# Crossbar transposes in an attention layer, from batch 2 on instead of batch 3

## The chip, the cores and the metric

One core of one Trainium2 chip. The metric is the device time of one execution in microseconds (us). Before the change was tried, the kernel took 334.17 us (median of 3 runs, 334.12 to 334.18). Every run in this document is in the fast state, in which executions of one kernel usually lie within 0.3%. The changed kernel's lie a little wider than the kernel before's; the experiments come back to that.

The engines go by their names in the profile: TensorE is PE, its weight loads PEld, VectorE is DVE, ScalarE ACT, GpSimd POOL and SyncE SP. PSUM is the memory that TensorE writes its results to. A DMA "lands" when its data has arrived; its landing time is counted from its issue.

## The reference

Attention over 8 batches of 8 heads, 576 positions, 64 dimensions per head, then a two-layer network over its result.

```
scores = q @ k^T / 8                       per batch and head
heads 0-3: keep 0 <= i - j < 32            ("local")
heads 4-7: keep j <= i, j = i (mod 32)     ("strided")
x   = softmax(scores) @ v                  -> [4608 tokens, 512]
h   = x @ w_in                             512 -> 2048
out = (max(h,0) + alpha*min(h,0)) @ w_out  2048 -> 512, float32
```

## The kernel before

The 4608 tokens go through the two layers in nine chunks of 512, each with 16 pieces of the first layer (64 matmuls of 512 columns) and 16 of the second (64 more). The attention is cut into pieces and threaded between them. Each batch has four head pairs, two local and two strided, numbered `g = 4*batch + pair`. `DX` is the batch from which the crossbar (a transposing DMA) takes over transposes from TensorE:

```
DX = 3
...
P.dx = P.b >= DX and P.strided      # q and k through the crossbar
P.xd = P.b >= DX and P.hp < 3       # results of pairs 0, 1, 2 through the crossbar
```

On the TensorE path q and k are transposed in eight matmuls each, plus four for the tail of the sequence, into PSUM, and DVE or ACT copies them on (`transpose_piece`, `tails`). On the crossbar path POOL loads q and k (casting to 16 bits) and SP issues the transposes:

```
def load_d(b):                                   # POOL queue, software DMA
    for nm, src in (("q", q), ("k", k)):
        keep(nc.gpsimd.dma_start(qks[nm][0:72], src[b, 4:8]...))
def transpose_d():                               # SP queue, crossbar
    for nm, dst in (("q", qTs[1]), ("k", kTs[1])):
        ...
        keep(nc.sync.dma_start_transpose(o, qks[nm]...))
```

`qks` is one pair of buffers, so a batch's load must wait until the crossbar has read the batch before. Results: on TensorE, `x_piece` transposes the pair into PSUM and a copy puts it into `xT`, the input of the first layer. On the crossbar path:

```
def x_dma(P):
    if P.strided:                                # pair 2: a scratch tile, then ACT reorders
        P.xs = xpool.tile([128, 8, 80], F16, ...)
        keep(nc.sync.dma_start_transpose(P.xs, P.x16[0:80, :]))
    else:                                        # pairs 0, 1: straight into xT
        keep(nc.sync.dma_start_transpose(xT[:, P.hp, ...], P.x16[0:96, 0:768]))
def x_copy(P):
    keep(nc.scalar.copy(xT[:, P.hp, ...], P.xs[:, :, 0:72]...))
```

Pair 3 of each batch stays on TensorE in both kernels; its copy on ACT is the last thing before the next chunk. The steps for pair `g` of batch `c` are tied to the attention pieces:

```
if lastp:
    if 4 * DX <= g - 1 < npair and pairs[g - 1].xd:
        x_dma(pairs[g - 1])
    if g % 4 == 0 and DX <= c < B:
        transpose_d()
    if g % 4 == 2 and DX <= c and c + 1 < B:
        load_d(c + 1)
    if g % 4 == 2 and c + 2 < B:
        load_v(c + 2, False)
if copyp and 4 * DX <= g - 2 < npair and pairs[g - 2].xd and pairs[g - 2].strided:
    x_copy(pairs[g - 2])
```

ACT's instructions stand in program order in the traces below: a wait of `x_copy` for the crossbar holds up whatever ACT has behind it. In the changed kernel an exponential whose scores were there at about 100.3 us ran at 102.86, behind such a wait.

The softmax here doesn't subtract the row's maximum and nothing guards it: scores larger than these inputs give would overflow.

Of the kernel before, what the change touches and what calls it, by code (L numbers as in the profile page):

```python
# [31 lines left out]
def kernel(  # L32
# [51 lines left out]

    NE = 6

    DX = 3
    qTs = [cpool.tile([128, 2, 672], F16, name=f"qT{i}") for i in range(2)]
    kTs = [cpool.tile([128, 2, 672], F16, name=f"kT{i}") for i in range(2)]
    vls = [cpool.tile([128, 24, 65], F16, name=f"vl{i}") for i in range(2)]  # L90
# [9 lines left out]
    def load_qk(b, strided, nm):  # L100



        h0 = 4 if strided else 0
        src = q if nm == "q" else k
        if strided and b:
            t16 = hpool.tile([128, 2, 512], F16, tag=f"{nm}s", bufs=3, name=f"{nm}s")
            cast16[(b, True, nm)] = t16
        else:
            t16 = hpool.tile([128, 2, 512], F32, tag=f"{nm}l", bufs=2, name=f"{nm}l")  # L110
            loaded[(b, strided, nm)] = t16
        base = src[b, h0 : h0 + 1, 0:1, :]
        eng = nc.sync if (b > 2 and not strided) or (b == 0 and strided) else nc.gpsimd
        keep(eng.dma_start(t16, bass.AP(
            tensor=base.tensor, offset=base.offset,
            ap=[[8 * D, 64], [2 * S * D, 2], [S * D, 2], [1, 8 * D]])))

    def load_d(b):

        for nm, src in (("q", q), ("k", k)):  # L120
            keep(nc.gpsimd.dma_start(
                qks[nm][0:72], src[b, 4:8, :, :].rearrange("h (p t) d -> p h (t d)", t=8)))

    def transpose_d():

        for nm, dst in (("q", qTs[1]), ("k", kTs[1])):
            o = dst.rearrange("r e c -> r (e c)")[:, 0:1280].rearrange("r (j p) -> r j p", p=80)
            keep(nc.sync.dma_start_transpose(o, qks[nm].rearrange("p h c -> p (h c)")))
# [6 lines left out]
    def cast_l(b, nm, eng="pool"):  # L135
        t16 = hpool.tile([128, 8, 2, 64], F16, tag=f"{nm}l16", bufs=2, name=f"{nm}l16")
        cast_copy(eng, t16, loaded[(b, False, nm)].rearrange("p f (t d) -> p t f d", t=8))
        cast16[(b, False, nm)] = t16

    def load_tail(b, strided):  # L140

        t16 = tpool.tile([128, 512], F16, tag="tl", name="tl16")
        for i, src in enumerate((q, k)):
            if strided:
                keep(nc.gpsimd.dma_start(
                    t16[32 * i : 32 * i + 32, :].rearrange("x (h c) -> x h c", h=4),
                    src[b, 4:8, 512:576, :].rearrange("h (x c) d -> x h (c d)", c=2)))
            else:
                keep(nc.gpsimd.dma_start(
                    t16[64 * i : 64 * i + 64, 0:256].rearrange("p (h d) -> p h d", h=4),  # L150
                    src[b, 0:4, 512:576, :].rearrange("h p d -> p h d")))
        cast16[(b, strided, "tail")] = t16

    def load_v(b, strided):


        if strided:
            st = spool.tile([128, 2048], F16, tag="v", bufs=2, name="stv")
            keep(nc.gpsimd.dma_start(
                st[0:72, :].rearrange("p (h e) -> p h e", h=4),  # L160
                v[b, 4:8, :, :].rearrange("h (p t) d -> p h (t d)", t=8)))
            loaded[b] = st
        else:
            v16 = vls[b % 2]
            base = v[b, 0:1, 0:1, :]
            r0 = 32 if b < 2 else 0
            keep(nc.gpsimd.dma_start(  # L167
                v16[r0:128, :, 0:64],
                bass.AP(tensor=base.tensor, offset=base.offset - (32 - r0) * D,
                        ap=[[D, 128 - r0], [96 * D, 24], [1, D]])))  # L170
            cast16[(b, False, "v")] = v16
# [30 lines left out]
    def make_pair(g):  # L202
# [5 lines left out]
        u = g // 2  # L208
        P.dx = P.b >= DX and P.strided
        P.xd = P.b >= DX and P.hp < 3  # L210
        if P.dx:
# [160 lines left out]
    def x_dma(P):  # L372
        base = (P.b % 4) * S
        if P.strided:
            P.xs = xpool.tile([128, 8, 80], F16, tag="xs", bufs=2, name="xs")
            keep(nc.sync.dma_start_transpose(P.xs, P.x16[0:80, :]))
        else:
            keep(nc.sync.dma_start_transpose(
                xT[:, P.hp, base : base + S].rearrange("r (w p) -> r w p", p=96), P.x16[0:96, 0:768]))
# [69 lines left out]
    for g in range(7, npair + 2):  # L449
# [3 lines left out]
        okP = 8 <= p < npair  # L453
        okT = 8 <= t < npair and (t % 4 == 0 or t < 4 * DX and t % 2 == 0)
        nP = len(pairs[p].pgroups) if okP else 0
# [27 lines left out]
        for i, (kind, fn) in enumerate(seq):  # L483
# [6 lines left out]
            def run(fn=fn, extra=extra, g=g, c=c, kind=kind, lastp=(i == lastP), copyp=(i == copyP)):  # L490
# [12 lines left out]
# [7 lines that stand above are left out]
# [103 lines left out]
    def load_unit(b, strided, v_too=True):  # L613
        load_qk(b, strided, "q")
        load_qk(b, strided, "k")
        load_tail(b, strided)
        if v_too:
            load_v(b, strided)
# [69 lines left out]
    load_tail(2, False)  # L688
    cast_l(1, "k")
    load_v(2, False)  # L690
    load_unit(2, True)
    cast_l(2, "q")
    cast_l(2, "k")

# [8 lines left out]
        attn_step(end1)  # L703
    wide["on"] = False
    load_unit(3, False)
    load_d(3)


    for n in range(1, NCH):
# [46 lines left out]
```

## Time and profile before

A chunk is measured in the chain (the work that ended last, followed backwards), from the place where its first layer starts to the place where the next chunk's does. The attention of batch 2 runs in chunk 1, which takes 39.09 us; that of batch 3, the first with the crossbar, in chunk 2, which takes 34.07. The lines that carry this are in the prediction. One more detail matters later: how a chunk ends. This is the chain of the kernel before at the end of chunk 1; the columns are start, length, what.

```profile
103.56 0.88 PE ops L586 x4
104.44 0.03 ACTq L591
104.47 0.04 issue
104.50 0.58 ACT osb L591
105.09 0.55 ACT xT L366
105.64 0.04 issue
105.68 2.10 PE hps L544 x9
```

TensorE's last matmul of the chunk is done at 104.44; ACT copies the output (`osb`), then pair 3's result (`xT`), and the next chunk starts in earnest 1.24 us later. Anything that makes ACT late here adds to that.

### The profile page before, as it was taken

The page shows a single profiled execution, that of the slowest core. Times are in us where ns is not written, and L with a number is a line of the kernel's source. Part 1 is how long each engine was busy: PE and PEld are TensorE (multiplying, and loading weights), DVE is VectorE, ACT ScalarE, POOL GpSimd, SP SyncE. Part 2 cuts the span into 40 slices and gives each one's busy share as a digit, 9 for nine tenths or more (in the row PEclk, how much of TensorE's full clock was granted, in tenths as well). Part 3 has the DMA queues.
Part 4 walks back from the last instruction along what each step waited for, and adds up shares of the span by engine and source line. Part 5 has one row for each costly group of instructions (what it writes and reads, how often), then busy time and mean ns, then how long its engine had stood idle before and what let it go on. Part 6 is the DMA issues. An engine that isn't in the chain of part 4 may idle for free.

```text
span 332.4 us, 6351 instructions
## 1 busy us (share of the span) xinstructions
PE 320.5 (96%) x2533; PEld 163.2 (49%) x2533; DVE 185.1 (56%) x363; ACT 172.5 (52%) x300; POOL 142.2 (43%) x154
## 2 busy tenths in 40 slices
PE   6899999999999999999999999999999999999995
PEld 2554455554554444444558754445444444444444
DVE  5477836477553873387428833784368337605800
ACT  2644753467535744575457644773476336425611
POOL 7932497137679365736483528332611400000000
PEclk9999999999999999999999999999999999999999
DMA  6999999399398649683979295715530120011011
GB/s 220 191 207 207 236 210 194 85 245 157 66 87 125 200 59 147 114 234 40 154 138 221 25 153 109 133 13 109 129 67 20 49 85 33 0 65 63 0 63 65
DMA packets 73117, 39.22 MB, mean 118 GB/s; under 512 B 54064, under 2 KB 64768, under 8 KB 73088
## 3 DMA queue, kind: packets, MB, share of 16 engines
q0 software_dynamic: 41760, 17.38, 48.7%
q1 hardware_dynamic: 31328, 21.44, 26.0%
q8 instruction: 20, 0.33, 0.4%
q14 instruction: 9, 0.07, 0.1%
HBM read 38.01 MB, written 9.44 MB: 143 GB/s over the span
## 4 chain that ended last, share of the span: by engine, by line
PE 89%; DVE 4%; ACT 3%; DMA 2%; issue 1%; SPq 0%; ACTq 0%
PE ops L586 37%; PE hps L544 36%; PE pv L345 4%; PE sp L295 4%; PE tp L235 3%; DMA ql<-in_q_dram 2%; DVE x L354 1%; PE wps L608 1%; PE ops L577 1%; ACT xT L366 1%; DVE qT L177 1%; ACT osb L591 1%; PE sp L311 1%; PE sph L311 1%; PE xp L362 1%
## 5 line engine op out<-in xcount | busy, mean ns | idle before, releaser
L586 PE MATMUL ops<-wout,gT 128*128 128x512 f16 x560 | 136.9, 379 | 0.2 <-DVE gT L557 0.2
L544 PE MATMUL hps<-xT,win 128*128 128x512 f16 (+1 forms) x640 | 134.3, 358 | 2.5 <-ACT xT L366 2.0
L557 DVE SCALAR_TENSOR_TENSOR gT<-neg,oma,hps 128x512 f16<-128x512 f32 x144 | 106.0, 744 | 49.8 <-ACT neg L554 42.2
L554 ACT ACTIVATE neg<-hps 128x512 f32<-128x512 f32 x144 | 86.0, 597 | 46.4 <-PE hps L544 45.2
L329 POOL TENSOR_TENSOR et<-et,consts 128x576 f16<-128x576 f16 (+1 forms) x48 | 61.1, 1274 | 95.4 <-ACT et L319 95.3
L544 PEld LDWEIGHTS <-win 128*128 128x128 f16 x640 | 59.4, 98 | 59.4 <-issue 6.1
L586 PEld LDWEIGHTS <-gT 128*128 128x128 f16 x560 | 48.3, 97 | 46.3 <-issue 0.5
L319 ACT ACTIVATE et<-sp 72x576 f16<-72x576 f32 (+1 forms) x56 | 36.1, 645 | 29.2 <-PE sp L295 15.3
L591 ACT COPY osb<-ops 128x512 f32<-128x512 f32 x35 | 20.5, 585 | 53.4 <-PE ops L586 49.6
L352 DVE RECIPROCAL rc<-pv 72x6 f32<-72x6 f32 (+2 forms) x80 | 14.9, 186 | 55.7 <-PE pv L345 55.6
L354 DVE TENSOR_TENSOR x<-pv,rc 96x384 f16<-96x384 f32 (+2 forms) x65 | 34.5, 531 | 2.2
L345 PEld LDWEIGHTS <-et 72*128 72x128 f16 (+1 forms) x448 | 23.4, 98 | 16.5 <-DVE x L354 1.1
L295 PEld LDWEIGHTS <-kT 64*128 64x128 f16 x448 | 10.8, 95 | 26.5 <-issue 21.2
L295 PE MATMUL sp<-qT,kT 64*128 64x72 f16 (+1 forms) x392 | 16.9, 201 | 1.9 <-ACT kT L175 1.7
L177 DVE COPY qT<-tp 128x1024 f16<-128x1024 f16 (+1 forms) x11 | 11.3, 1030 | 12.3 <-PE tp L235 12.3
L608 PE MATMUL wps<-wrm 128*128 128x512 f16 x44 | 15.7, 428 | 1.2 <-DVE wrm L620 1.2
L167 POOL DMA_DIRECT2D vl<-in_v_dram x8 | 11.1, 1394 | 10.7 <-PE xp L362 9.1
L345 PE MATMUL pv<-vs,et 72*128 72x65 f16 x256 | 15.3, 194 | 0.1
L179 POOL COPY vs<-stv 72x1024 f16<-72x1024 f16 x14 | 14.3, 1032 | 0.0
L175 ACT COPY kT<-tp 128x1024 f16<-128x1024 f16 (+1 forms) x11 | 9.4, 858 | 8.4 <-PE tp L235 8.4
L345 PE MATMUL pv<-vl,et 128*128 128x65 f16 x192 | 11.1, 194 | 0.0
L383 ACT COPY xT<-xs 128x576 f16<-128x576 f16 x5 | 6.5, 1301 | 5.2 <-DMA xs<-x16s 5.2
(73 smaller groups left out, 169.5 us busy)
## 6 DMA issues: line engine op xcount, KB each, us to landing
out_dram<-osb SPq DMA_DIRECT2D x35, 256.0 KB, 2.3
ql<-in_q_dram SPq DMA_DIRECT2D x6, 512.0 KB, 5.5
kl<-in_k_dram SPq DMA_DIRECT2D x6, 512.0 KB, 6.6
stv<-in_v_dram POOLq DMA_DIRECT2D x8, 288.0 KB, 6.2
vl<-in_v_dram POOLq DMA_DIRECT2D x6, 384.0 KB, 9.8
win<-in_moe_w_in_dram POOLq DMA_DIRECT2D x4, 512.0 KB, 10.1
wout<-in_moe_w_out_dram POOLq DMA_DIRECT2D x4, 512.0 KB, 17.1
ql<-in_q_dram POOLq DMA_DIRECT2D x3, 512.0 KB, 8.9
```

Of the source, the lines that this page charges most:

```text
L295: keep(nc.tensor.matmul(sps[y][:, w * x : w * x + w], P.kT[hf, k0 : k0 + 128], P.qT[hf, q0 : q0 + w], start=(x == 0), stop=(x == len(grp) ...
L319: keep(nc.scalar.activation(ev.rearrange("r (y c) -> r y c", y=2), sp[0:r, :, 0:n], AF.Exp, scale=SCALE))
L329: keep(nc.gpsimd.tensor_tensor(ev, ev, m, op=ALU.mult))
L345: keep(nc.tensor.matmul(pv[:, 65 * x : 65 * x + 65], et[0:r, c : c + 128], v16[0:r, 2 * P.pr + hh, t, :] if P.strided else v16[:, 6 * (2 * ...
L352: keep(nc.vector.reciprocal(rc[0:w, 0:nb], pvv[:, :, 64]))
L354: keep(nc.vector.tensor_tensor(P.x16[0:w, c0 : c0 + 64 * nb].rearrange("r (c e) -> r c e", e=64), pvv[:, :, 0:64], rc[0:w, 0:nb].unsqueeze ...
L544: keep(nc.tensor.matmul(hps[:, dst : dst + w], win16[:, kk, 128 * m : 128 * m + 128], xT[:, kk, src : src + w], start=(kk == 0 and x == 0) ...
L554: keep(nc.scalar.activation(neg, hps, AF.Relu, scale=-1.0))
L557: keep(nc.vector.scalar_tensor_tensor(gTs[n][:, m, :], neg, oma[:, m : m + 1], hps, op0=ALU.mult, op1=ALU.add))
L586: keep(nc.tensor.matmul(ops, gTs[n][:, kf, 128 * mt : 128 * mt + 128], wout16[:, kf, :], start=(kf == 0), stop=(kf == 15)))
L591: keep(nc.scalar.copy(osb, ops))
L608: keep(nc.tensor.matmul(wps, wrm[:, 0:128], wrm, start=True, stop=True))
```

## The change

It lets batch 2 use the crossbar too. Its intent is to take 40 small transposes, with their PSUM copies, off TensorE, DVE and ACT.

```
-    DX = 3
+    DX = 2
...
     load_v(2, False)
-    load_unit(2, True)        # q, k, tails and v of batch 2, strided, for TensorE
+    load_d(2)                 # q and k for the crossbar
+    load_v(2, True)
...
     load_unit(3, False)
-    load_d(3)                 # batch 3's crossbar loads, early (66 us)
```

The last line is not decoration: with one pair of buffers, batch 3's loads can't come before batch 2's crossbar has read them. By the schedule above they now come at `g = 10`, in the middle of chunk 1.

## The prediction

> **What bounds the kernel now.** I read the page first (engine busy shares and the chain that ended last), then the chain in order of time, then the busy time of each engine in the stretches that the chain shows, and last the waits.
>
> ```profile
> PE 320.5 (96%) x2533; PEld 163.2 (49%) x2533; DVE 185.1 (56%) x363; ACT 172.5 (52%) x300; POOL 142.2 (43%) x154
> ...
> PE 89%; DVE 4%; ACT 3%; DMA 2%; issue 1%; SPq 0%; ACTq 0%
> ```
>
> The chain is 89% TensorE; no other engine is busy over 56%. Two instruction groups carry it, the 128x512 matmuls of the two linear layers (L544 and L586, 37% and 36% of the span). In the chain 4 of them take 0.86 us, 0.216 each. Nine chunks of 128 such matmuls are 9 x 128 x 0.216 = 249 us of 332: three quarters of the time is work that this change doesn't touch. The rest is attention work of TensorE that is threaded between those matmuls, and a few gaps. So a TensorE instruction that is taken out between two such matmuls is worth its own place in the chain, and work on other engines is worth nothing unless it opens or closes a gap.
>
> The stages follow from the chain: the first matmul of each chunk's first layer starts at 27.16, 66.59, 105.68, 139.75, 173.81 us and so on. The attention of batch 2 runs inside the chunk from 66.59 to 105.68 (chunk 1), that of batch 3, which already uses the crossbar, largely in chunk 2.
>
> ```profile
> 66.59:105.68 39.09, 38.45 (x350) 19.82 (x350) 23.99 (x47) 22.87 (x40) 26.66 (x28) 1.00 0.85 135
> 105.68:139.75 34.07, 33.68 (x267) 16.15 (x267) 19.75 (x38) 19.45 (x32) 20.17 (x21) 1.00 0.99 129
> 139.75:173.81 34.06, 33.79 (x271) 16.55 (x271) 19.76 (x38) 19.27 (x32) 18.96 (x19) 1.00 1.08 143
> ```
>
> The columns are length, then busy time (and instructions) of PE, PEld, DVE, ACT and POOL, the granted clock, DMA share, GB/s. Chunk 1 is 5.0 us longer than its successors at the same clock, and TensorE is busy in nearly all of it (38.45 of 39.09): it has more TensorE work, not more waiting. Only part of that surplus is what the change removes: the chunk also fills the attention pipeline (the local transposes of batch 2 and several score pieces beyond a steady chunk's), and that stays.
>
> **What the Trainium skill says.** (1) "Perfetto Trace Analysis", section Identifying the Most-Contended Engine: matmul busy time does not tell how near TensorE is to its limit, because matmuls are pipelined. The trace agrees: the 128x512 matmul has a mean record of 379 ns but advances the chain by 216 ns. So I size everything by places in the chain, not by mean durations. (2) "TensorE: Matmul & The Clock Gate", section Part 4: PE-mode transpose: some 275 ns for a 128x128 transpose inside a kernel, and the result lands in PSUM, so a copy follows. The trace has the copies, but not the price: the record is 219 ns, and eight transposes take 0.45 us of the chain, 56 ns each. The measurement decides. (3) "DMA: Bandwidth & Descriptors", section DMA Transpose (X-bar): it is issued by SP or ACT and writes to SBUF, so the PSUM copy goes too; all of this kernel's are issued by SP, one stream. (4) Same page, section Issuing engines are not separate DMA queues: all DMAs share 16 engines and interleave. The trace agrees: q and k loads of the crossbar path land in 5.8 and 7.0 us at the median, but in 14.8 and 15.9 when issued at 66.6 us beside some 2 MB of other loads.
>
> **The change part by part.** The lines of the chain in chunk 1 that are TensorE work of the strided half of batch 2, or of its three results, with the gaps beside them:
>
> ```profile
> 75.61 0.29 issue
> 75.90 0.66 ACT et L319
> ...
> 79.74 0.75 DVE gT L557
> ...
> 81.84 1.13 DVE qT L177
> 82.97 0.67 DVE gT L557
> ...
> 84.89 0.45 PE tp L235 x8
> 85.33 0.22 PE tt L258 x4
> ...
> 88.01 0.26 PE xp L362 x6
> ...
> 93.22 0.26 PE xp L362 x6
> ...
> 99.53 0.26 PE xp L362 x8
> ```
>
> Removed from TensorE. (a) Eight q transposes; in the PE timeline they stand at 80.82 us, where the chain happens to run over DVE, and like the eight k transposes (0.45 in the chain) they take 0.45. (b) Eight k transposes, 0.45. (c) Four tail transposes, 0.22. (d) The result transposes of the two local pairs and of the first strided pair, 0.26 each, 0.78. The sum is 0.45 + 0.45 + 0.22 + 0.78 = 1.90 us and 40 matmuls with their 40 weight loads; the built order agrees (80 rows of TensorE fewer). Of this 1.45 us (b, c, d) lies in the second layer of the chunk, from 83.7 us on, where the chain goes over TensorE from end to end: it comes off in full.
>
> Removed elsewhere. DVE loses a 1.2 us copy of q, two small tail copies (0.34) and two result copies (0.44 each); ACT loses the k copy (1.01), two tail copies (0.34), and one result copy of 0.65 is replaced by one of 1.30 from the crossbar's result. None of this lengthens the chain, but it closes gaps in the first layer of the chunk. Between 66.59 and 83.64 us, 17.05 us, I count TensorE work of 63 x 0.216 = 13.6, three groups of eight transposes 1.35, two tails 0.11, four score pieces 0.92 plus 0.11 of refill after each, and one value piece 0.18: 16.6. So about 0.44 us are gaps: about 0.25 before the score piece at 76.60, which needs the exponential that started at 75.90, and 0.18 before 83.68, where TensorE needed a DVE result that was queued behind the q copy. In the new order eight matmuls, not four, lie between the first two score pieces, which covers the first gap; the q copy is gone, which closes the second. I count 0.35 of the 0.44.
>
> Added. Two crossbar transposes of q and k (SP is busy with issuing 1.35 and 1.9 to 4.4 us), three of results (1.2 us each), one crossbar result copy on ACT. Moved: the loads for batch 3's crossbar leave 66.6 us and come in the middle of chunk 1, 1.5 us of POOL issue between masks that have several us until they are used. Loads of batch 2 keep their bytes (two of 288 KB in place of two of 256 and two of 32 KB). None of it is TensorE work.
>
> Sum: 1.90 + 0.35 = 2.25 us; 334.17 - 2.25 = 331.9 us. Chunk 1 should take about 36.8 us, every other chunk what it takes now.
>
> **The rivals.** First: the crossbar of q and k is late and its wait takes the place of the transposes. In the new SP order the two follow the q and k loads of batch 3, issued at 65.9 and 66.7 us, so they are issued near 67 and 69, and the first strided scores stand some 18 us after the chunk's start, near 84.7. At the landing times of the existing ones (3.8, 6.5, 7.5 us least, median, most) that is 8 us early; at the 10.8 us of the k loads in this stretch still about 4 early. Only the 15.9 us of a load issued from POOL here would make TensorE wait, by about 1 us: then 333. Second: the transposes of batch 3 become late, because their loads move from 66.6 to about 88 us. Their transposes are issued near 98.4 (100.68 now, less 2.3) and wait for those loads, which at the median land at 95 to 96; the scores that read them start near 109.4, and now they land about 2 us before that. A load as slow as 15 us would cost some 4 us and leave a time of 334 to 336; but the DMA share from 84 to 92 is 0.17 to 0.30, and later chunks run in this rhythm with no such wait in the list. Third: the result copy on ACT waits for the crossbar (5.2 us in 2 of the 5 cases now) and holds back exponentials behind it. TensorE did not wait for it in chunks 2 to 6; worth 0.3 us at most. Fourth: all of the surplus of chunk 1 goes, 5 us, which gives 329. The count of instructions (40 of a surplus of 83) speaks against it.
>
> **Range and chances.** The 1.90 are sure within 0.2, the gaps are worth 0 to 0.7, and the rivals pull upward: 8 times in 10 the time is between 331.3 and 332.9 us, most likely 331.9, a change of 0.7%. Faster by over 2% needs less than 327.5, 4.4 us below the sum, more than everything the chunk has in surplus: 1 in 100. Slower by over 2% needs a wait of 9 us from a transpose: 1 in 100. Within 2%: 98 in 100.
>
> **What would show it right or wrong.** Right: chunk 1 shrinks to about 36.8 us with its start unmoved at 66.6; 40 matmuls fewer; transposes of strided q and k on TensorE remain for batches 0 and 1 alone; the chain from 83 us on stays on TensorE; later chunks keep 34.06 us. The gaps step is wrong if the first layer of chunk 1 shrinks by only 0.45 us or by more than 0.9. The first rival shows as TensorE waiting for a DMA into qT or kT near 85 us; the second as the same near 110, with a chunk 2 longer than 34.1; the third as ACT idle before its crossbar copy near 99 us together with TensorE idle before a score piece. If chunk 0 changes by over 0.2 us, the DMA load of batch 2 mattered and I overlooked it.

## The result

| | median, us | range, us | runs |
|---|---|---|---|
| before | 334.18 | 333.87 to 334.32 | 6 |
| changed | 332.94 | 332.49 to 333.40 | 6 |

The ratio is 0.9964, 95% interval 0.9951 to 0.9977. Ratios here are the mean time of one kernel's fast runs over that of the other's of the same rounds, so they are not quite the ratio of the medians. The kernel gains 1.24 us; 2.25 were predicted, and 332.94 lies just outside the range of 331.3 to 332.9.

The stretches of the changed kernel (chunks 1, 2, 3; columns as in the prediction):

```profile
66.59:104.56 37.97, 36.52 (x310) 18.14 (x310) 21.97 (x42) 22.30 (x37) 26.32 (x27) 1.00 1.18 168
104.56:138.63 34.07, 33.68 (x267) 16.16 (x266) 19.75 (x38) 19.28 (x32) 20.45 (x21) 1.00 0.95 131
138.63:172.69 34.06, 33.79 (x271) 16.56 (x271) 19.75 (x38) 19.28 (x32) 19.02 (x19) 1.00 1.03 142
```

Chunk 1 starts where it did and has exactly 40 matmuls fewer (310 for 350), at the same clock. It is 1.12 us shorter, not 2.3; chunks 2 and 3 are unchanged. So what is missing is inside chunk 1. TensorE's idle time says it too: 39.09 - 38.45 = 0.64 us before, 37.97 - 36.52 = 1.45 us now. The end of the chunk in the chain shows where:

```profile
101.38 0.88 PE ops L586 x4
102.26 0.03 ACTq L591
102.28 0.57 issue
102.86 0.64 ACT et L319
103.50 0.47 ACT osb L591
103.97 0.55 ACT xT L366
104.52 0.04 issue
104.56 2.10 PE hps L544 x9
```

TensorE is through at 102.26, which is 2.18 us earlier than before (104.44). But from there to the start of the next chunk it takes 2.30 us instead of 1.24: 1.06 us are given back. In front of the output copy there is now an exponential (`et`) that in the kernel before was done 0.5 us before it. ACT's own timeline tells why; the columns are start, length, instruction, shapes, count and, in brackets, how long the engine idled before it and for what. Before:

```profile
101.00 0.65 ACT L319 ACTIVATE et<-sp 128x576 f16<-128x576 f32 x1 [0.30 <-PE sp L295]
103.37 0.65 ACT L319 ACTIVATE et<-sp 128x576 f16<-128x576 f32 x1 [1.73 <-PE sp L295]
104.50 0.58 ACT L591 COPY osb<-ops 128x512 f32<-128x512 f32 x1 [0.48 <-PE ops L586]
```

Changed:

```profile
98.14 0.66 ACT L319 ACTIVATE et<-sp 128x576 f16<-128x576 f32 x1
101.64 1.31 ACT L383 COPY xT<-xs 128x576 f16<-128x576 f16 x1 [2.85 <-DMA xs<-x16s]
102.86 0.64 ACT L319 ACTIVATE et<-sp 128x576 f16<-128x576 f32 x1
103.40 0.57 ACT L591 COPY osb<-ops 128x512 f32<-128x512 f32 x1
```

ACT stands for 2.85 us before its copy of the strided pair's crossbar result (`xs`). The exponential behind it, whose scores were in PSUM by about 100.3, runs at 102.86; the output copy and pair 3's copy come after that. The crossbar is late, and much runs beside it. The DMA queues from 94 to 98 us in the changed kernel (for each queue packets, MB, and the added-up time of its packets as a share of the 16 DMA engines' time, which can exceed 100%; then an issue in that stretch with the microseconds to landing):

```profile
q0 software_dynamic: 2739, 0.54, 164.8%
q1 hardware_dynamic: 46, 0.09, 9.7%
...
xs<-x16s SPq DMA_TRANSPOSE x1, 5.6
```

It was issued at 96.0 us and took 5.6 us; the five `xs` crossbars of the kernel before took 2.7 at the median and 3.7 at most. In these 4 us the software queue, which POOL's loads use, moved 0.54 MB, and the hardware queue, which the crossbar uses, 0.09. That the one holds up the other is at this point an inference; the experiments test it. Among those loads are the ones that the change moved there: `load_d(3)` is issued at 88.9 and 89.6 us and lands 6.5 and 7.7 us later, and `load_v` behind it takes 10.5 us, for 6.8 before.

### The profile page after: what moved, and what is told of

It reads as the page before. It is cut to its first block, busy times and chain, and to the rows that moved or that the text cites. A ratio compares the mean times of both kernels' runs of the same rounds, so it can differ in the third digit from the quotient of the medians.

```text
span 331.5 us, 6272 instructions
## 1 busy us (share of the span) xinstructions
PE 319.1 (96%) x2493; PEld 161.6 (49%) x2493; DVE 183.0 (55%) x358; ACT 171.8 (52%) x297; POOL 141.2 (43%) x152
## 3 DMA queue, kind: packets, MB, share of 16 engines
HBM read 38.01 MB, written 9.44 MB: 143 GB/s over the span
## 4 chain that ended last, share of the span: by engine, by line
PE 89%; ACT 4%; DVE 3%; DMA 2%; issue 1%; SPq 0%; ACTq 0%
PE hps L544 37%; PE ops L586 37%; PE sp L295 4%; PE pv L345 4%; PE tp L235 2%; DMA kl<-in_k_dram 2%; DVE x L354 1%; PE wps L608 1%; PE ops L577 1%; ACT xT L366 1%; ACT osb L591 1%; PE sph L311 1%; PE sp L311 1%; ACT kT L175 1%; DVE qT L177 1%
## 5 line engine op out<-in xcount | busy, mean ns | idle before, releaser
L354 DVE TENSOR_TENSOR x<-pv,rc 96x384 f16<-96x384 f32 (+2 forms) x62 | 33.0, 532 | 2.1
L177 DVE COPY qT<-tp 128x1024 f16<-128x1024 f16 (+1 forms) x10 | 10.1, 1010 | 11.7 <-PE tp L235 11.7
L167 POOL DMA_DIRECT2D vl<-in_v_dram x8 | 11.2, 1396 | 11.8 <-PE xp L362 10.5
L175 ACT COPY kT<-tp 128x1024 f16<-128x1024 f16 (+1 forms) x10 | 8.4, 843 | 7.4 <-PE tp L235 7.4
L383 ACT COPY xT<-xs 128x576 f16<-128x576 f16 x6 | 7.8, 1302 | 7.6 <-DMA xs<-x16s 7.6
```

The lines of the kernel that those rows point to most:

```text
L354: keep(nc.vector.tensor_tensor(P.x16[0:w, c0 : c0 + 64 * nb].rearrange("r (c e) -> r c e", e=64), pvv[:, :, 0:64], rc[0:w, 0:nb].unsqueeze ...
```

## The experiments

**Theory A**: the moved loads of batch 3 delay the strided pair's crossbar; ACT waits for it in order; so pair 3's copy and the next chunk are late. **Theory B**: a crossbar result at this place costs this anyway, with its 1.3 us copy; the loads don't matter. **Theory C**, a smaller question: whether it is the exponential or only the copies behind the wait that count.

All experiments gave correct results. The quoted text under each is what was expected, on record before the run. The table has the profiled execution of each but two_buffers, early_late and early_dve, which follow in the text; "chunk 1" is measured in the chain as above.

| run | `xs` lands after, us | ACT waits for it, us | chunk 1, us | median, us (range) |
|---|---|---|---|---|
| changed | 5.6 | 2.85 | 37.97 | 332.94 (332.49 to 333.40) |
| changed, again | 5.7 | 2.90 | 38.01 | 332.48 (332.41 to 333.39) |
| early_load | 4.0 | 1.24 | 36.90 | 332.24 (332.03 to 334.81) |
| early_load, again | 4.5 | 1.69 | 36.91 | 332.28 (332.05 to 332.93) |
| pair_on_pe | no such crossbar | none | 37.10 | 332.21 (332.17 to 332.36) |
| late_copy | 5.1 | none recorded | 36.91 | 332.35 (332.25 to 332.53) |
| extra_load | 7.0 | 4.22 | 39.33 | 336.31 (334.96 to 337.33) |
| qk_only | no such crossbar | none | 37.51 | 332.81 (332.70 to 332.95) |
| results_only | 2.8 | 0.28 | 37.97 | 333.31 (332.79 to 333.72) |

### The loads one pair earlier (early_load)

```
-    if g % 4 == 2 and DX <= c and c + 1 < B:
+    if g % 4 == (1 if c == DX else 2) and DX <= c and c + 1 < B:
         load_d(c + 1)
```

> Changed kernel, but the crossbar loads of batch 3 (qsd, ksd) are issued one pair earlier (near 84 us instead of 88.9), where the DMA engines are nearly idle. Theory A (the changed kernel loses some 1 us at the end of chunk 1 because the crossbar of the strided result pair lands late, 5.6 us, behind those loads, and ACT waits for it in order): the crossbar lands in about 3 to 4 us, ACT waits under 1 us instead of 2.85, the time falls by 0.7 to 1.0 us to about 332.0. Theory B (the wait comes from the crossbar and its 1.3 us ACT copy as such, loads don't matter): the time stays at 332.9.

Ratio to before 0.9951 (0.9936 to 0.9965), median 332.24; one of the ten runs took 334.81, the rest at most 332.46. The crossbar lands in 4.0 us, ACT still waits 1.24 us (under 1 was expected; 1.69 in the repetition), and the chunk is 1.07 us shorter than the changed kernel's, to the point where ACT is just in time: the chain goes from TensorE to the output copy again.

```profile
101.28 0.53 PE ops L586 x3
101.81 0.42 issue
102.22 0.58 ACT osb L591
102.81 0.55 ACT xT L366
103.36 0.04 issue
103.40 2.10 PE hps L544 x9
```

### The loads at their old place, with buffers of their own (two_buffers)

```
-    qks = {nm: cpool.tile([80, 4, 512], F16, ...) for nm in "qk"}
+    qkss = [{nm: cpool.tile([80, 4, 512], F16, ...) for nm in "qk"} for i in range(2)]
...
     load_unit(3, False)
+    load_d(3)
```

> Changed kernel, but q and k of batch 3 for the crossbar have buffers of their own and are loaded at 66 us, as in the kernel before. Theory A: no such loads near 96 us, the result crossbar lands in about 3 us, time about 332.0. Theory B: 332.9. A side risk: the q and k crossbars of batch 2 share 66 to 83 us with these loads; if they land after 85 us TensorE waits for them and the time is 333 or more.

It got slower: 337.38 us (336.02 to 340.64), ratio 1.0119 (1.0081 to 1.0158). The end of chunk 1 took 1.24 us again: the `xs` crossbar landed in 2.6 us and ACT didn't wait. But the crossbar also came 5 us later (101.1 us), past most of the other loads, so this is no clean test of Theory A. The side risk came true. In TensorE's timeline (this kernel's line numbers are two higher) the first strided scores of batch 2 wait for k's crossbar, issued at 72.0 us, which took 16.7 us to land, for 9.8 in the changed kernel:

```profile
88.71 0.42 PE L297 MATMUL sp<-qT,kT 64*128 64x72 f16 x8 [3.26 <-DMA kT<-ksd]
```

So both places are bad for these loads, each for another crossbar: at 66 us they delay q and k, at 89 us the result. This is the prediction's first rival, which doesn't occur in the changed kernel only because the loads moved: there q and k landed 11.8 and 9.8 us after 67.4 and 70.8, at 79.2 and 80.6, and the scores start at 85.1.

### The strided pair back on TensorE (pair_on_pe)

```
-    P.xd = P.b >= DX and P.hp < 3
+    P.xd = P.b >= DX and P.hp < (2 if P.b == DX else 3)
```

> Changed kernel, but the strided result pair of batch 2 goes back to TensorE (eight transposes, 0.26 us, ACT copy 0.65 instead of 1.30 us); the other parts of the change stay. Theory A and B alike: the ACT wait is gone, the chunk end costs 1.24 us again instead of 2.30, so 1.06 less and 0.26 more: about 332.1 us. If the time stays at 332.9, the late crossbar is not what holds the end of chunk 1.

332.21 us, ratio 0.9943 (0.993 to 0.9956): doing 0.26 us more on TensorE made the kernel faster than the changed one. The spread of its five runs is 0.19 us. The changed kernel's eleven runs (here and in the repetition below) range over 1 us, from 332.41 to 333.40. Kernels without this crossbar in batch 2 are steady (ranges of 0.19 us in pair_on_pe, 0.25 in qk_only), as far as five runs tell; several of those that have it vary by 0.9 us or more. The wait can't be the only source of that: results_only, below, has the crossbar and almost no wait in its profile, and still ranges over 0.93 us. Both profiled runs of the changed kernel, 333.40 and 333.39 us, were the slowest of their set, so the traces show its bad case. That the wait is shorter in its faster runs is plausible, but no trace shows one.

### ACT's copy one exponential later (late_copy)

```
-    if copyp and 4 * DX <= g - 2 < npair and pairs[g - 2].xd and ...strided:
+    if copyp and g - 2 != 10 and 4 * DX <= g - 2 < npair and ...strided:
         x_copy(pairs[g - 2])
+    if kind == "S" and g == 13:
+        x_copy(pairs[10])
```

> Changed kernel, but the ACT copy of the crossbar result of batch 2 stands one exponential later in ACT's order. Theory A says that ACT's in-order wait is what costs: the exponential goes ahead at 100.5 us, the copy starts when the crossbar has landed (101.6) and delays the output copy and the last result copy by some 0.6 us instead of 1.06: about 332.5 us. Theory C (the exponential doesn't matter, the copies behind it do): the same 332.5 or no change, so this run sizes the order alone.

332.35 us, ratio 0.9948 (0.9936 to 0.9959). The crossbar was still late (5.1 us), but with the exponential in front ACT came to the copy just as it landed, at 101.04, and chunk 1 took 36.91 us:

```profile
101.06 1.31 ACT L383 COPY xT<-xs 128x576 f16<-128x576 f16 x1
```

ACT's order thus takes part in turning a late DMA into lost time. How much, this run doesn't say cleanly, as the crossbar also landed some 0.6 us earlier than in the changed kernel's profile (101.04 for about 101.6). By estimate from these two profiles, the landing at 101.6 would have left about 0.5 us of the 1.06 lost, as was expected. Theory C stays open.

### One more load of the same kind (extra_load)

```
         load_d(c + 1)
+        if c == DX:
+            keep(nc.gpsimd.dma_start(spare[0:72], v[7, 4:8, :, :]...))   # 288 KB, not used
```

> Dose: changed kernel with one more load of 288 KB of the same kind (into an unused buffer; the result stays right) right behind batch 3's crossbar loads. Theory A: the strided pair's crossbar lands later than 5.6 us, by some 3 us; ACT and with it the end of chunk 1 wait that much longer: 335 to 336 us. Theory B: 332.9, at most 333.2.

336.31 us, ratio 1.0061 (1.0039 to 1.0083). ACT in its profile:

```profile
102.99 1.30 ACT L384 COPY xT<-xs 128x576 f16<-128x576 f16 x1 [4.22 <-DMA xs<-x16s]
104.20 0.65 ACT L320 ACTIVATE et<-sp 128x576 f16<-128x576 f32 x1
104.74 0.58 ACT L595 COPY osb<-ops 128x512 f32<-128x512 f32 x1
```

The crossbar lands 1.4 us later than the changed kernel's (some 3 were expected), ACT waits 1.37 us longer, chunk 1 takes 1.36 us longer. The profiled run was again not typical, here the fastest (334.96); what the other three lost beyond it no trace shows.

### Each part alone (qk_only, results_only)

```
qk_only:       -  P.xd = P.b >= DX and P.hp < 3      +  P.xd = P.b > DX and P.hp < 3
results_only:  (from the kernel before, DX = 3)      +  P.xd = P.b >= 2 and P.hp < 3
```

In results_only the two conditions on `4 * DX` become `8` as well, so that `x_dma` and `x_copy` run for batch 2; batch 3's loads stay at 66 us.

> One part alone: q and k of the strided half of batch 2 by crossbar, all results of batch 2 by TensorE as before. Removes 20 transposes, 0.45 + 0.45 + 0.22 = 1.12 us of the chain, and adds no crossbar that the end of chunk 1 waits for: 1.1 to 1.4 us off, 332.8 to 333.0 us (by my count of gaps 332.9).

> The other part alone: three result pairs of batch 2 by crossbar, q and k by TensorE, batch 3's crossbar loads at 66 us as before. Removes 20 transposes, 0.78 us of the chain. Theory A: with those loads out of the way the crossbar of the strided pair lands in 3 to 4 us and ACT waits under 1 us, so the full 0.8 us come off: 333.4 us. Theory B (any crossbar result here is late): most of it is lost, 333.9 to 334.3.

qk_only: 332.81 us, ratio 0.9959 (0.9947 to 0.9972). results_only: 333.31 us, ratio 0.9973 (0.9962 to 0.9984). Both lie where they were expected. Against 334.18, the gains are 1.37 and 0.87 us, together 2.24; the whole change gains 1.24 (1.70 in its repetition below). That 2.24 is so near the predicted 2.25 is partly luck: in the profiles chunk 1 shrinks by 1.58 and 1.12 us, together 2.70, where the whole change has TensorE through 2.18 us earlier. Part of that surplus counts twice, as each part alone cuts TensorE's idle time in the first layer from 0.27 to 0.09 us; the rest is not explained. The clean comparison is the end of chunk 1, from TensorE's last matmul to the next chunk: 1.24 us in each part alone, 2.30 in the whole. That 1.06 is lost only where both parts meet: the first brings loads to 89 us, the second a crossbar behind them. In results_only, where the loads stay away, the crossbar lands in 2.8 us, and ACT waits 0.28:

```profile
99.91 1.30 ACT L383 COPY xT<-xs 128x576 f16<-128x576 f16 x1 [0.28 <-DMA xs<-x16s]
```

That is Theory A; Theory B, which had predicted 333.9 or more there, falls.

### The changed kernel again, with the repairs beside it (after_again, early_again, early_late)

The last combines early_load and late_copy.

> The changed kernel once more, for a comparison within the same rounds. About 332.9 us with a spread of near 1 us, as before; the strided pair's crossbar lands in 5 to 6 us, ACT waits 2.5 to 3 us.

> The kernel of early_load once more, in the same rounds as the changed kernel. Theory A: 332.2 us, 0.6 to 0.9 below the changed kernel. Theory B: no difference.

> early_load and late_copy together: the loads come earlier and ACT's copy of the crossbar result stands behind one more exponential. If the two repair the same loss, they don't add up: 332.0 to 332.3 us, with a smaller spread than the changed kernel. If they repair different ones, 331.6.

In the same rounds: 332.48 (ratio 0.9952, 0.9939 to 0.9966), 332.28 (0.9945, 0.9933 to 0.9958) and 332.31 us (332.01 to 332.35; ratio 0.994, 0.9928 to 0.9953). The difference of the first two was expected to be 0.6 to 0.9 and is 0.2 between the medians: three of the changed kernel's five runs lay at the fast end of its range this time (332.41 to 332.48). The intervals overlap, so the timed runs of this set alone don't prove the repair. The profiles show it, for the changed kernel's slow runs: chunk 1 is 38.01 us in the one and 36.91 in the other. Early loads and late copy don't add up: chunk 1 takes 36.91 us with both in early_late, as with either alone, so they repair the same loss.

### A version that beats both (early_dve)

early_load, and from batch 2 on pair 3's copy on DVE, which idles there, instead of ACT behind the output copy:

```
+    copy = nc.vector.tensor_copy if P.b >= 2 else nc.scalar.copy
-    keep(nc.scalar.copy(
+    keep(copy(
         xT[:, P.hp, ...], xp[:, 0:576]...))
```

> Candidate: the earlier loads as in the run early_load, and from batch 2 on the last pair's result copy from PSUM goes from ACT to the idle DVE, where it need not stand behind the 0.58 us output copy. In each of the five or six chunk ends the chain shows output copy 0.58 then result copy 0.55 on ACT; if the copy on DVE takes no longer, each end loses some 0.55 us: 332.2 - 5.5 x 0.55 = 329.2 us. If the chain's wait at the chunk ends is for something else, 332.2.

331.40 us (331.10 to 331.59), ratio 0.9916 (0.9903 to 0.993): the fastest here, but 0.8 us gained instead of 3. The chain shows the chunk's end is now

```profile
102.20 0.28 PE xp L362 x8
102.48 0.02 issue
102.50 0.77 DVE xT L367
103.27 0.04 issue
103.31 2.10 PE hps L545 x9
```

From TensorE's last matmul of the second layer to the next chunk it takes 1.11 us, for 1.24: pair 3's transposes on TensorE (0.28), which the output copy had covered, now count, and DVE's copy takes 0.77 of the chain where ACT's took 0.55. The wait at a chunk's end was as described, but the copy on DVE is not as short.

## Why the prediction was wrong

- **What bounds the kernel.** Right: TensorE's chain, places of 0.216 us, chunk 1.
- **1.90 us of transposes.** Right, for each part: TensorE is through with chunk 1 2.18 us earlier, and the parts alone gain 1.37 (1.12 and a share of the gaps expected) and 0.87 us (0.78 expected).
- **0.35 us of gaps.** Too large, and made good by luck. The first layer of the chunk shrank by 0.55 us (from 17.09 to 16.54) for 0.45 + 0.35 = 0.80 expected, so its gaps gave 0.10: the two gaps named were closed, but the first scores now wait 0.17 us for ACT's copy of k, and TensorE's idle time there fell just from 0.27 to 0.20. The second layer, up to TensorE's last matmul, gave 1.63 for 1.45; idle time there was 0.03 us before, so these 0.18 are not gaps, and the prediction doesn't have them. The sum is 2.18 for 2.25 because two errors cancel.
- **First rival** (q and k late). It didn't happen: landing 4.5 us ahead of the scores, "about 4 early" was said. In two_buffers it happened and cost more than foreseen, as k's crossbar took 16.7 us there.
- **Second rival** (batch 3's crossbar late). It didn't happen: issued at 98.7 and 101.3 us, landed 6.7 and 6.8 us later, at 105.4 and 108.1; the scores came at 110.6, chunk 2 kept its 34.07.
- **Third rival: the step that failed.** The prediction named it ("waits for the crossbar ... and holds back exponentials behind it") and sized it "0.3 us at most", because chunks 2 to 6 of the kernel before showed no harm. It cost 1.06 us at the end of chunk 1 in the profile. The path was also another than said: TensorE did not stop before a score piece, but at the next chunk's first layer, for the output copy and pair 3's copy that stood behind the exponential on ACT. Three things were overlooked. Those chunks were a weak precedent: their crossbars landed in 2.7 us at the median and 3.7 at most, the new one in 5.6. Chunk 1 is denser in attention work and leaves less time between the loads at `g = 10` and the crossbar at `g = 11`, 7.1 us in the changed kernel, for 10.4 between batch 4's loads and batch 3's crossbar in chunk 2. And the prediction followed the moved loads only to the transposes that read them, and POOL's issue time only to the masks; it didn't ask which other DMA would be in flight beside them. "None of it is TensorE work" was true and not enough.
- **Range.** "Within 2%" came true. The 8-in-10 range was too narrow on the upper side: with 1.06 added, the same sum gives 334.17 - 2.25 + 1.06 = 333.0 us, and the median measured was 332.94. That they agree so well is luck too: the 1.06 comes from a profiled run of 333.40. The miss is small: the repetition's median of 332.48 lies in the range, and so does that of all eleven runs, 332.83. The step failed in the profiles of both sets all the same (1.06 and 1.11 us).

In the profiled runs a further 0.2 us is lost after TensorE's last matmul: the span ends 3.79 us after it in the changed kernel (331.5 less 327.71) and 3.56 before (332.4 less 328.84). Other profiled runs have it too (3.74 in early_load); I have no cause for it.

## What to carry to other kernels

When a change moves a DMA, list what else is in flight in the stretch that it moves to, above all small transfers whose landing an in-order engine waits for; a queue with room on average can still double one landing. Then read what stands behind that wait on the waiting engine: putting the waiting instruction one place later can be worth as much as making the transfer fast. And run the parts of a change alone: what the whole has and neither part alone shows, here 1.06 us at one chunk's end, is their interaction.

## What the Trainium skill lacked or had wrong

- "TensorE: Matmul & The Clock Gate", Part 4: PE-mode transpose, gives about 275 ns for a 128x128 transpose within a kernel. Here the record of one is 219 ns, and queued ones take 0.45 us for eight, 56 ns each, in the chain.
- The same page, Back-to-back issue gap, says that sustained pairs of weight load and matmul reach about 131 ns at 512 columns. Here 64 such pairs in a row take 13.81 us, 216 ns each, with the clock granted in full; that is the figure the page has for an isolated gap.
- "DMA: Bandwidth & Descriptors", DMA Transpose (X-bar), has no landing times beside other traffic. A result crossbar here (80 x 1024 elements of 16 bits) landed in 2.6 to 2.8 us with few loads beside it, in 4.0 to 5.7 us beside more loads on the software queue and in 7.0 with one load of 288 KB more; those of q and k took 3.8 to 16.7 us.
